# Attention results through DRAM instead of transposes, and a new order of the attention loop

## The chip, the cores and the metric

The kernel runs on one core of one Trainium2 chip. The metric is the device time in microseconds (us) of one execution; lower is better. In the texts PE is the tensor engine, DVE the vector engine, ACT the scalar engine, POOL the GpSimd engine and SP the engine that issues most DMAs.

## The reference

Four layers in a row on one sequence of 2048 rows of 512 values: attention, MLP, attention, MLP, with the same weights both times. Each adds its result to its input, which goes in normalised.

```
def _A_ref(x, wqkv, wo):                 # attention, H = 32 heads of 16
    qkv = (x @ wqkv) ...                 # split into q, k, v by heads
    scores = einsum("bhqd,bhkd->bhqk", q, k) * 16 ** -0.5
    p = softmax(scores)
    o = einsum("bhqk,bhkd->bhqd", p, v)
    return o.reshape(B, S, D) @ wo
def _B_ref(x, w1, b1, w2):               # 512 -> 1792, Mish, -> 512
    ...
x = x + _A_ref(_layernorm(x), A_wqkv, A_wo)
x = x + _B_ref(_layernorm(x), B_w1, B_b1, B_w2)
x = x + _A_ref(_layernorm(x), A_wqkv, A_wo)
x = x + _B_ref(_layernorm(x), B_w1, B_b1, B_w2)
```

## The kernel before, in words

The text speaks of a "layer" for one attention with its MLP; there are two (l = 0 and 1).

**Precision.** Values of large matmuls are split into a high and a low part of a fast format (`mm3`: three matmuls for one product), so weights and activations are stored twice, after a copy and a subtraction ("split"). p x v works on plain float32 tiles.

**The attention loop** (`Attention.run`) goes over 512 steps. A step stands for one block of 512 queries, one tile of 128 keys and four heads. 16 steps (all keys) make a block, four blocks (all queries) a group of four heads, and eight groups all heads. There are 2048 head tiles in a layer, 3 of them to one `p` tile. What is done in a step is listed letter by letter in `CYCLE`, which repeats every three steps:

- P (`pair`): two matmuls give the scores of two head tiles in one two-bank PSUM tile (tag s2, one buffer), and one exp on ACT of 1024 columns writes them to `p`. After each P, `drain` looks whether a block is finished.
- S (`single`): the third head tile, one bank (tag s1, one buffer), an exp of 512 columns.
- M (`max_mm`): half of what one step needs for the row maxima: two matmuls into a PSUM tile of 1024 columns (tag mx, two buffers) and a max reduce on DVE. 1024 halves make a layer. They run ahead of the scores, by 24 steps at the start (`AHEAD`; these are made during the q, k, v projection). At the end of a block `max_fold` and, three steps later, `max_rows` bring the maxima with one transpose on PE into two additional rows of the queries, so that the scores come out shifted.
- v (`pv`): p x v, four heads side by side in 32 columns each of the array, accumulated over the 16 steps of a block in one PSUM bank (tag acc, one buffer). Each head has 32 columns: 16 of v, one of ones (for the sum of p), the rest zero.

PE's instructions are chained in this program order by `pe`. The order on the other engines, and the slots of the pools, are chosen when the program is built by a scheduler with a time model; each engine and the queue of SP then hold their instructions in that order.

**The end of a block.** `drain` copies the accumulator to SBUF on ACT (`ot`, L360). Two steps later `out_rows` transposes it on PE (L368), copies it again, inverts the sums with a pow on POOL (L373) and writes the normalised result to the tiles `ost` (four tiles of 8 KB per partition that stay for the whole attention).

**The tail.** `wo_parts` transposes these tiles (L495), splits them and multiplies by wo, chunk by chunk (a chunk is 512 rows, c = 0 to 3); chunk 0 is spread over the last 24 steps of the loop ("fill"), in PE's chain. Behind the loop follow the other chunks, the splits of the remaining w1 and w2 (`load_w1`, `load_w2`, with `split_load`: a DMA into one of three raw buffers, a copy on DVE, a subtraction on POOL), the norm of the first chunk, and the MLP.

**SBUF.** Nearly all large tiles come from one pool, `blk`, of 22 slots of 8 KB per partition: q and k of a group (four slots), v of a group, the `p` tiles, weights and residuals. A DMA into such a tile waits in SP's queue until its slot is free.

The lines of the profile's code that the change touches:

Of the kernel before, what the change touches and what calls it, by code (L numbers as in the profile page):

```python
# [25 lines left out]
HG = 4  # L26
# [8 lines left out]
HALF = 64  # L35
K_PARTS = (0, 0, 1)
Q_PARTS = (0, 1, 0)
CYCLE = ("PMSvv", "PMSvMPMSv", "PMSvvM")
AHEAD = 24
GSTEPS = NCH * NKT  # L40
STEPS = NG * GSTEPS
# [8 lines left out]
def kernel(ctx: ExitStack, tc: tile.TileContext, x, wqkv, wo, w1, b1, w2, out):  # L50
# [15 lines left out]
    mone = const.tile([P, NCH * HG], F32, name="mone")  # L66
    nc.gpsimd.memset(mone, -1.0)
# [113 lines left out]
    class Attention:  # L181
        def __init__(self, l, scr):
            self.l, self.scr = l, scr
            self.vscr = dram.tile([NG, P, NKT, HG * VW], F32, name=f"vscr{l}")
            self.va = {}
            self.qk, self.mxs, self.pts, self.accs = {}, {}, [], {}
            self.singles, self.full = 0, None
            self.ost = None
            self.later = []
            self.chained, self.running, self.last = False, False, None  # L190

# [133 lines left out]
            self.pe(nc.tensor.matmul(sp, k, q, start=True, stop=True))  # L325
            nc.scalar.activation(self.pts[i // 3][:, 2], sp, AF.Exp, scale=SCALE)  # L326

        def pv(self, i):
            s, half = divmod(i, 2)
            if not 0 <= s < STEPS:  # L330
                return
            b, kt = divmod(s, NKT)
            g, qb = divmod(b, NCH)
            l = self.l
            va = self.va[g]
            if kt == 0 and half == 0:
                self.accs[b] = pbank("acc", f"pv{l}{b}")
            acc = self.accs[b]
            cols = ts(half, CW // 2)
            for h in range(HG):  # L340
                j, e = divmod(s * HG + h, 3)
                self.pe(
                    nc.tensor.matmul(  # L343
                        acc[ts(h, VW), cols],
                        va[:, kt, h, :],
                        self.pts[j][:, e, cols],
                        start=kt == 0 and half == 0,
                        stop=kt == NKT - 1,
                        skip_group_check=True,
                    )  # L350
                )
            if kt == NKT - 1 and half == 1:
                self.full = b

        def drain(self):
            b, self.full = self.full, None
            if b is None:
                return
            ot = t512("f", f"ot{self.l}{b}")
            nc.scalar.activation(ot, self.accs.pop(b), AF.Copy)  # L360
            self.later.append((2, lambda: self.out_rows(b, ot)))

        def out_rows(self, b, ot):
            g, qb = divmod(b, NCH)
            l = self.l
            tp = self.bank(f"otp{l}{b}")
            for t in range(NCH):
                self.pe(nc.tensor.transpose(tp[:, ts(t, P)], ot[:, ts(t, P)], ident))  # L368
            of = t512("f", f"of{l}{b}")
            nc.scalar.activation(of, tp, AF.Copy)  # L370
            ov = of.rearrange("p (t h d) -> p t h d", t=NCH, h=HG)
            rc = tmp.tile([P, NCH, HG, 1], F32, tag="rc", name=f"rc{l}{b}")
            nc.gpsimd.tensor_tensor(  # L373
                rc, ov[:, :, :, DH : DH + 1], mone.rearrange("p (t h o) -> p t h o", t=NCH, h=HG), op=ALU.pow
            )
            nc.gpsimd.tensor_tensor(
                self.ost[qb][:, :, ts(g, HG * DH)].rearrange("p t (h d) -> p t h d", d=DH),
                ov[:, :, :, 0:DH],
                rc.to_broadcast([P, NCH, HG, DH]),
                op=ALU.mult,  # L380
            )

        def run(self, hooks, ost, fill):
            ost.extend(b8([P, NCH, D], F32, f"o{self.l}{c}") for c in range(NCH))
            self.ost = ost
# [36 lines left out]
    def qkv(l, wts, tt, order, late):  # L422
# [65 lines left out]
    def wo_parts(l, c, ost, wot, x2, pe, tail):  # L488
        def rows(t):
            if tail:  # L490
                tp = ps.tile([P, 2, 512], F32, tag="mx", name=f"op{l}{c}{t}")[:, 0]
            else:
                tp = pbank("s", f"op{l}{c}{t}")
            for k in range(KT):
                pe(nc.tensor.transpose(tp[:, ts(k, P)], ost[:, t, ts(k, P)], ident))  # L495
            oh = t512("ah", f"oh{l}{c}{t}", F32R)
            ol = t512("al", f"ol{l}{c}{t}", F32R)
            if tail:
                nc.vector.tensor_copy(oh, tp)
            else:  # L500
                nc.scalar.activation(oh, tp, AF.Copy)
            nc.vector.tensor_tensor(ol, tp, oh.bitcast(F32), op=ALU.subtract)
            return oh, ol

        ready = rows(0)
        yield
        for t in range(NCH):
            oh, ol = ready
            if t % 2 == 0:
                acc = ps.tile([P, 2, 512], F32, tag="mx", name=f"wo{l}{c}{t}")  # L510
            for k in range(KT):
                mm3(
                    acc[:, t % 2],
                    [(oh[:, ts(k, P)], ol[:, ts(k, P)], wot[k // 2][:, 0, k % 2], wot[k // 2][:, 1, k % 2])],
                    first=k == 0,
                    last=k == KT - 1,
                    pe=pe,
                )
                yield
                if k == 0 and t + 1 < NCH:  # L520
                    ready = rows(t + 1)
                    yield
# [88 lines left out]
    for l in range(2):  # L611
# [21 lines left out]
        for i in range(2):  # L633
            hooks[STEPS - GSTEPS + 2 * i] = lambda i=i: wot.append(load_rows(wo, i, f"wo{l}{i}", hi="pool"))
            hooks[STEPS - 40 + i] = lambda i=i: load_res(i)
        for i in range(4):
            hooks[STEPS - GSTEPS + 8 + 2 * i] = lambda i=i: load_w1(i, hi="pool")
        ost = []

        def wo_first():  # L640
            yield from wo_parts(l, 0, ost[0], wot, x2s[0], att.pe, True)

        fill = wo_first()
        att.run(hooks, ost, fill)
# [56 lines left out]
```

## Time and profile before

| | |
|---|---|
| median of 3 runs | 3804.7 us (3803.79 to 3808.43) |
| the profiled execution, its own time | 3797.65 us |
| its span, first to last instruction | 3795.9 us |
| granted PE clock, mean | 0.994 |
| q, k, v projection, layer 0 | to about 200 us |
| attention, layer 0 (first p x v to last) | 207.8 to 1538.1 us |
| wo matmuls, layer 0 | 1470.6 to 1586.2 us |
| MLP, layer 0 (first to last matmul) | 1577.2 to 1932.6 us |
| attention, layer 1 | 2092.5 to 3425.2 us |
| MLP, layer 1 | 3468.2 to 3791.1 us |

The two attentions take 70% of the time. The busy share of an engine over the whole span mixes stages, so what one stage waits for has to be read in that stage. In the groups of instructions, "idle before" is idle time of that engine ahead of the group, with what ended it; idle time of an engine that is not the one all others wait for costs nothing.

### The profile page before, as it was taken

The page shows a single profiled execution, that of the slowest core. Times are in us where ns is not written, and L with a number is a line of the kernel's source. Part 1 is how long each engine was busy: PE and PEld are TensorE (multiplying, and loading weights), DVE is VectorE, ACT ScalarE, POOL GpSimd, SP SyncE. Part 2 cuts the span into 40 slices and gives each one's busy share as a digit, 9 for nine tenths or more (in the row PEclk, how much of TensorE's full clock was granted, in tenths as well). Part 3 has the DMA queues.
Part 4 walks back from the last instruction along what each step waited for, and adds up shares of the span by engine and source line. Part 5 has one row for each costly group of instructions (what it writes and reads, how often), then busy time and mean ns, then how long its engine had stood idle before and what let it go on. Part 6 is the DMA issues. An engine that isn't in the chain of part 4 may idle for free.

```text
span 3795.9 us, 70660 instructions
## 1 busy us (share of the span) xinstructions
PE 3681.6 (97%) x29504; PEld 2050.2 (54%) x29504; DVE 3008.9 (79%) x3010; ACT 2558.6 (67%) x3573; POOL 746.6 (20%) x594
## 2 busy tenths in 40 slices
PE   7999999999999999999999999999999999999999
PEld 5644444444444444687767444444444444447887
DVE  5679999999999995566655899999999999946555
ACT  2178888888888887444431788888888888873444
POOL 1200100100110030444420010010011001305544
PEclk9999999999999999999999999999999999999999
DMA  6530111102011110100055202111020110101000
GB/s 193 178 70 21 27 24 36 27 21 36 22 27 29 31 35 23 62 12 12 28 167 184 40 22 38 19 30 30 18 36 21 32 32 23 57 1 62 12 12 23
DMA packets 108849, 168.16 MB, mean 44 GB/s; under 512 B 13808, under 2 KB 61936, under 8 KB 102384
## 3 DMA queue, kind: packets, MB, share of 16 engines
q1 hardware_dynamic: 86288, 122.73, 14.0%
q10 hardware_dynamic: 22240, 40.90, 3.1%
q8 instruction: 232, 3.80, 0.4%
q14 instruction: 89, 0.73, 0.1%
HBM read 102.77 MB, written 58.72 MB: 43 GB/s over the span
## 4 chain that ended last, share of the span: by engine, by line
PE 83%; ACT 8%; DVE 3%; DMA 2%; POOL 1%; issue 1%; SPq 0%; ACTq 0%; POOLq 0%; DVEq 0%
PE pv L343 25%; PE pm L261 16%; PE sp L315 12%; PE ss L325 8%; ACT p L316 5%; PE h L133 2%; PE mo L135 2%; PE h L135 2%; PE h L134 2%; PE mo L133 2%; PE mo L134 2%; ACT p L326 1%; PE qk L133 1%; PE qk L134 1%; PE qk L135 1%
## 5 line engine op out<-in xcount | busy, mean ns | idle before, releaser
L265 DVE TENSOR_REDUCE mxv<-pm 128x2 f32<-128x1024 f32 x2048 | 2423.4, 1221 | 299.7 <-PE pm L261 292.1
L316 ACT ACTIVATE p<-sp 128x1024 f32<-128x1024 f32 x1366 | 1398.2, 1024 | 454.0 <-PE sp L315 443.3
L343 PE MATMUL pv<-p,va 128*32 128x256 f32 x16384 | 1168.9, 388 | 0.0
L261 PE MATMUL pm<-ks,qs 48*128 48x512 f32 x4096 | 916.1, 446 | 4.4 <-DMA qs<-scr 3.2
L326 ACT ACTIVATE p<-ss 128x512 f32<-128x512 f32 x1364 | 809.5, 593 | 0.0
L343 PEld LDWEIGHTS pv<-p,va 128*32 128x32 f32 x16384 | 393.8, 109 | 564.6 <-issue 426.3
L315 PE MATMUL sp<-qs,ks 50*128 50x512 f32 x2732 | 623.5, 451 | 18.6 <-ACT p L316 9.5
L261 PEld LDWEIGHTS pm<-ks,qs 48*128 48x128 f32 x4096 | 384.9, 185 | 369.1 <-issue 267.9
L325 PE MATMUL ss<-qs,ks 50*128 50x512 f32 x1364 | 551.9, 405 | 5.2 <-ACT of L370 0.6
L373 POOL TENSOR_TENSOR rc<-of,mone 128x16 f32<-128x16 f32 x64 | 186.3, 2912 | 1485.1 <-ACT of L370 1432.6
L315 PEld LDWEIGHTS sp<-qs,ks 50*128 50x128 f32 x2732 | 259.3, 184 | 317.9 <-ACT p L316 266.8
L325 PEld LDWEIGHTS ss<-qs,ks 50*128 50x128 f32 x1364 | 253.9, 186 | 127.9 <-ACT p L326 56.2
L546 POOL TENSOR_TENSOR hb<-hb,he 128x512 f32<-128x512 f32 x112 | 157.5, 1406 | 186.9 <-DVE he L543 180.1
L288 POOL CAST np<-nf 16x128 fp32r<-16x128 f32 x64 | 17.9, 280 | 893.7 <-ACT nf L287 880.1
L549 POOL TENSOR_TENSOR hb<-hb,hr 128x512 f32<-128x512 f32 x112 | 161.1, 1439 | 136.9 <-DVE ah L548 113.3
L133 PE MATMUL mo<-w,ah 128*128 128x512 f32 x448 | 178.9, 399 | 0.8 <-DVE ah L548 0.7
L544 ACT ACTIVATE hr<-he 128x512 f32<-128x512 f32 x112 | 70.9, 633 | 159.5 <-DVE he L543 81.0
L133 PE MATMUL h<-thm,w 128*128 128x512 f32 x448 | 176.1, 393 | 1.4 <-ACT hb L540 1.4
L134 PE MATMUL mo<-w,ah 128*128 128x512 f32 x448 | 176.8, 395 | 0.0
L550 DVE TENSOR_TENSOR al<-hb,ah 128x512 fp32r<-128x512 f32 x112 | 110.8, 989 | 83.1 <-POOL hb L549 80.2
L135 PE MATMUL h<-thm,w 128*128 128x512 f32 x448 | 175.7, 392 | 0.0
L134 PE MATMUL h<-tlm,w 128*128 128x512 f32 x448 | 175.3, 391 | 0.0
(170 smaller groups left out, 2982.0 us busy)
## 6 DMA issues: line engine op xcount, KB each, us to landing
scr<-pt ACTq DMA_DIRECT2D x64, 512.0 KB
qs<-scr SPq DMA_DIRECT2D x192, 128.0 KB
ks<-scr SPq DMA_DIRECT2D x192, 128.0 KB
vscr<-v SPq DMA_DIRECT2D x32, 512.0 KB
va<-vscr SPq DMA_DIRECT2D x64, 256.0 KB
qs<-np SPq DMA_DIRECT2D x512, 2.0 KB
x<-in_A_x_dram SPq DMA_DIRECT2D x7, 1024.0 KB
xs<-x SPq DMA_DIRECT2D x4, 1024.0 KB
```

Of the source, the lines that this page charges most:

```text
L133: pe(nc.tensor.matmul(acc, ah, bh, start=first and i == 0, stop=False))
L134: pe(nc.tensor.matmul(acc, ah, bl, start=False, stop=False))
L135: pe(nc.tensor.matmul(acc, al, bh, start=False, stop=last and i == n - 1))
L261: nc.tensor.matmul(pm[:, e], qs[u][rows, q0 : q0 + P], ks[u][rows, ts(n, 512)], start=True, stop=True)
L265: nc.vector.tensor_reduce(self.mxs[b][:, 2 * u : 2 * u + 2, qt, n], pm, axis=AX.X, op=ALU.max)
L315: self.pe(nc.tensor.matmul(sp[:, e], k, q, start=True, stop=True))
L316: nc.scalar.activation(self.pts[-1][:, 0:n], sp[:, 0:n], AF.Exp, scale=SCALE)
L325: self.pe(nc.tensor.matmul(sp, k, q, start=True, stop=True))
L326: nc.scalar.activation(self.pts[i // 3][:, 2], sp, AF.Exp, scale=SCALE)
L343: nc.tensor.matmul(acc[ts(h, VW), cols], va[:, kt, h, :], self.pts[j][:, e, cols], start=kt == 0 and half == 0, stop=kt == NKT - 1, skip_g ...
L373: nc.gpsimd.tensor_tensor(rc, ov[:, :, :, DH : DH + 1], mone.rearrange("p (t h o) -> p t h o", t=NCH, h=HG), op=ALU.pow)
L549: nc.gpsimd.tensor_tensor(hb, hb, r, op=ALU.mult)
```

## The change

- `CYCLE` gets a new order. p x v is done in four groups per three steps, each of 384 columns (three quarters of 128), where it was done in six halves of 256. A group that crosses from one step to the next is issued in two pieces. At a block's end the group breaks off until the accumulator has been drained, and the next one takes up what was left.
- The list of M changes with the order: `"PMSvv", "PMSvMPMSv", "PMSvvM"` becomes `"PMvSM", "PvMSMPv", "MSMPvMS"`.
- `drain` no longer transposes. The block's raw result (values and sums of four heads) goes to DRAM (`oscr`) by a DMA on SP. All 16 unused columns of a head's v are filled with ones now, so that the sum comes out 16 times, once for each value.
- `heads_out` reads a chunk back with 16 DMAs, in which the heads' dimension lies on the partitions, as the wo matmuls want it: values and sums in two tiles. DVE makes a reciprocal over 2048 columns and a multiply; ACT copies the high part, DVE subtracts for the low part. It is called for chunk 0 at step 482, for chunk 1 at step 503, for chunks 2 and 3 behind the loop.
- `wo_parts` no longer transposes or splits. The four `ost` tiles are gone. One w1 tile instead of four is loaded and split during the attention; the other three follow behind wo's chunk 0, with the high part on DVE.

```diff
-CYCLE = ("PMSvv", "PMSvMPMSv", "PMSvvM")
+CYCLE = ("PMvSM", "PvMSMPv", "MSMPvMS")
+QW = CW // 4
...
+            self.oscr = [dram.tile([KT, 2, P, CW], F32, name=f"oscr{l}{c}") for c in range(NCH)]
...
-        def pv(self, i):
-            s, half = divmod(i, 2)
...
+        def pv(self, upto):
+            while self.unit < min(upto, 4 * STEPS):
+                s, q0 = divmod(self.unit, 4)
+                q1 = min(4, upto - 4 * s)
+                b, kt = divmod(s, NKT)
+                if kt == 0 and q0 == 0:
+                    if self.full is not None:
+                        return
+                    self.accs[b] = pbank("acc", f"pv{self.l}{b}")
+                cols = slice(q0 * QW, q1 * QW)
+                for h in range(HG):
...
+                self.unit = 4 * s + q1
+                if kt == NKT - 1 and q1 == 4:
+                    self.full = b
...
             ot = t512("f", f"ot{self.l}{b}")
             nc.scalar.activation(ot, self.accs.pop(b), AF.Copy)
-            self.later.append((2, lambda: self.out_rows(b, ot)))
-
-        def out_rows(self, b, ot):
...
+            nc.sync.dma_start(self.oscr[qb][g // 2, g % 2], ot)
...
-                for s in range(STEPS + 2):
+                for s in range(STEPS + 4):
...
                         else:
-                            self.pv(done)
                             done += 1
+                            self.pv(3 * done)
...
-                    nc.gpsimd.memset(v, 0.0)
-                    nc.gpsimd.memset(v[:, :, :, DH : DH + 1], 1.0)
+                    nc.gpsimd.memset(v, 1.0)
...
+    def heads_out(l, c, src):
+        nd = []
+        for a in range(2):
+            t = b8([P, KT, CW], F32, f"nd{l}{c}{a}")
+            for hh in range(P // DH):
+                rows = src[c].rearrange("k g (h r) n -> k (g h) r n", r=VW)[:, hh, a * DH : (a + 1) * DH]
+                nc.sync.dma_start(t[ts(hh, DH)], rows.rearrange("k d n -> d k n"))
+            nd.append(t)
+        num, den = nd
+        nc.vector.reciprocal(den, den)
+        nc.vector.tensor_tensor(num, num, den, op=ALU.mult)
+        oh = b8([P, KT, CW], F32R, f"oh{l}{c}")
+        ol = b8([P, KT, CW], F32R, f"ol{l}{c}")
+        nc.scalar.activation(oh, num, AF.Copy)
+        nc.vector.tensor_tensor(ol, num, oh.bitcast(F32), op=ALU.subtract)
+        return oh, ol
...
-        for i in range(4):
-            hooks[STEPS - GSTEPS + 8 + 2 * i] = lambda i=i: load_w1(i, hi="pool")
-        ost = []
+        hooks[STEPS - GSTEPS + 8] = lambda: load_w1(0, hi="pool")
+        outs = {}
...
+        hooks[STEPS - 30] = lambda: finish(0)
+        hooks[STEPS - 9] = lambda: finish(1)
...
         for c in range(NCH):
-            for _ in fill if c == 0 else wo_parts(l, c, ost[c], wot, x2s[c], lambda ins: ins, False):
+            if c + 2 < NCH:
+                finish(c + 2)
+            for _ in fill if c == 0 else wo_parts(l, c, outs, wot, x2s[c], lambda ins: ins):
                 pass
             if c == 0:
-                for i in range(4, 7):
+                for i in range(1, 7):
                     load_w1(i, hi="dve")
```

More of the change, by code (lines that the diff above doesn't have):

```diff
@@ L184, in __init__ @@
             self.vscr = dram.tile([NG, P, NKT, HG * VW], F32, name=f"vscr{l}")
+            self.oscr = [dram.tile([KT, 2, P, CW], F32, name=f"oscr{l}{c}") for c in range(NCH)]
             self.va = {}
             self.qk, self.mxs, self.pts, self.accs = {}, {}, [], {}
-            self.singles, self.full = 0, None
-            self.ost = None
+            self.singles, self.full, self.unit = 0, None, 0
             self.later = []
@@ L326, in single @@
             nc.scalar.activation(self.pts[i // 3][:, 2], sp, AF.Exp, scale=SCALE)
-        def pv(self, i):
-            s, half = divmod(i, 2)
[L330 to L349, printed above, removed]
-                    )
-                )
-            if kt == NKT - 1 and half == 1:
-                self.full = b
+        def pv(self, upto):
[9 more added lines that the diff above has]
+                for h in range(HG):
+                    j, e = divmod(s * HG + h, 3)
+                    self.pe(
+                        nc.tensor.matmul(
+                            self.accs[b][ts(h, VW), cols],
+                            self.va[b // NCH][:, kt, h, :],
+                            self.pts[j][:, e, cols],
+                            start=kt == 0 and q0 == 0,
+                            stop=kt == NKT - 1,
+                            skip_group_check=True,
+                        )
+                    )
+                self.unit = 4 * s + q1
+                if kt == NKT - 1 and q1 == 4:
+                    self.full = b
         def drain(self):
@@ L358, in drain, with run @@
                 return
+            g, qb = divmod(b, NCH)
             ot = t512("f", f"ot{self.l}{b}")
             nc.scalar.activation(ot, self.accs.pop(b), AF.Copy)
-            self.later.append((2, lambda: self.out_rows(b, ot)))
-        def out_rows(self, b, ot):
[L364 to L385, printed above, removed]
+            nc.sync.dma_start(self.oscr[qb][g // 2, g % 2], ot)
+        def run(self, hooks, fill):
             self.prep_v(0)
@@ L486, in qkv, with wo_parts @@
         return att
[L488 to L506, printed above, removed]
+    def heads_out(l, c, src):
[14 more added lines that the diff above has]
+        return oh, ol
+    def wo_parts(l, c, outs, wot, x2, pe):
+        oh, ol = outs[c]
         for t in range(NCH):
-            oh, ol = ready
             if t % 2 == 0:
@@ L519, in wo_parts @@
                 yield
-                if k == 0 and t + 1 < NCH:
-                    ready = rows(t + 1)
-                    yield
             if t % 2:
@@ L635, with finish @@
             hooks[STEPS - 40 + i] = lambda i=i: load_res(i)
-        for i in range(4):
-            hooks[STEPS - GSTEPS + 8 + 2 * i] = lambda i=i: load_w1(i, hi="pool")
-        ost = []
+        hooks[STEPS - GSTEPS + 8] = lambda: load_w1(0, hi="pool")
+        outs = {}
+        def finish(c):
+            outs[c] = heads_out(l, c, att.oscr)
+        hooks[STEPS - 30] = lambda: finish(0)
+        hooks[STEPS - 9] = lambda: finish(1)
         def wo_first():
-            yield from wo_parts(l, 0, ost[0], wot, x2s[0], att.pe, True)
+            yield from wo_parts(l, 0, outs, wot, x2s[0], att.pe)
         fill = wo_first()
-        att.run(hooks, ost, fill)
+        att.run(hooks, fill)
         for c in range(NCH):
-            for _ in fill if c == 0 else wo_parts(l, c, ost[c], wot, x2s[c], lambda ins: ins, False):
+            if c + 2 < NCH:
+                finish(c + 2)
+            for _ in fill if c == 0 else wo_parts(l, c, outs, wot, x2s[c], lambda ins: ins):
                 pass
             if c == 0:
-                for i in range(4, 7):
+                for i in range(1, 7):
                     load_w1(i, hi="dve")
```

4 lines of the change are left out of this document (1 added, 3 removed).

## The prediction

> **What bounds the kernel now.** I read the page first, then the table by stage, the groups and the timeline. The sums are made against the profiled execution (3797.65 us, a span of 3795.9 us and 1.75 us around it); the median of the runs is 7 us above it, and I add those at the end.
>
> ```profile
> PE 3681.6 (97%) x29504; PEld 2050.2 (54%) x29504; DVE 3008.9 (79%) x3010; ACT 2558.6 (67%) x3573; POOL 746.6 (20%) x594
> ```
> ```profile
> 400.00:1200.00 800.00, 786.65 (x7521) 366.68 (x7513) 732.64 (x638) 646.19 (x883) 80.74 (x76) 1.00 0.15 27
> ```
> ```profile
> L265 DVE TENSOR_REDUCE mxv<-pm 128x2 f32<-128x1024 f32 x2048 | 2423.4, 1221 | 299.7 <-PE pm L261 292.1
> L373 POOL TENSOR_TENSOR rc<-of,mone 128x16 f32<-128x16 f32 x64 | 186.3, 2912 | 1485.1 <-ACT of L370 1432.6
> ```
>
> The second line is 800 us of attention: columns are PE, weight loads, DVE, ACT, POOL, clock. PE is busy 98% at full clock, but DVE 92%, so two engines stand within a few per cent of the bound. Its 638 DVE instructions are 619 reduces (one fold, L276, per 32), so 1.29 us per reduce and 7.76 us per three steps of six reduces. How close can reduces stand?
>
> ```profile
> 829.08 0.61 ACT L360 ACTIVATE ot<-pv 128x512 f32<-128x512 f32 x1
> ...
> 829.55 1.05 ACT L316 ACTIVATE p<-sp 128x1024 f32<-128x1024 f32 x1
> 829.74 1.07 PE L343 MATMUL pv<-p,va 128*32 128x256 f32 x16
> ...
> 831.28 2.36 DVE L265 TENSOR_REDUCE mxv<-pm 128x2 f32<-128x1024 f32 x2 [0.41 <-PE pm L261]
> ...
> 833.15 0.66 PE L368 MATMUL otp<-ident,ot 128*128 128x128 f32 x4 [0.20 <-ACT p L326]
> ...
> 839.92 5.95 DVE L265 TENSOR_REDUCE mxv<-pm 128x2 f32<-128x1024 f32 x5 [0.34 <-PE pm L261]
> ```
>
> A pair of reduces takes 2.36 us, five 5.95, one alone 1.22: the next starts 1.14 us (2.36-1.22) to 1.18 us ((5.95-1.22)/4) after the one before. Where no max is left, the score bank sets the pace:
>
> ```profile
> 1528.96 1.02 ACT L316 ACTIVATE p<-sp 128x1024 f32<-128x1024 f32 x1 [0.17 <-PE sp L315]
> ...
> 1530.65 1.02 ACT L316 ACTIVATE p<-sp 128x1024 f32<-128x1024 f32 x1 [0.17 <-PE sp L315]
> ```
>
> One P every 1.69 us: a pair's scores wait for its bank until the exp before has ended.
>
> **Part 1: seven maxes per three steps.** The new CYCLE holds 4 P, 4 S, 4 v, and 2+2+3 = 7 M where the old one held 6. The 1024 halves of a layer start 48 ahead as before, so 976 are left, and they are used up at 976x3/7 = step 418 of 512 (the old list: step 488). PE would need little more: v stays six sets of matmuls, 1536 columns and four changes in and out; one M adds 0.24 us, the output transposes go (0.66 us and some 0.5 us of waits per 16 steps, 0.2 us per three steps). So PE can keep 7.8 us. DVE cannot: 7 x (1.17 + 0.007 for folds) = 8.24 us. Each M has two buffers, and PE's order is fixed, so PE waits at M and everything behind it waits. Steps 0 to 418: 976 x 1.177 = 1149 us.
>
> **Part 2: the drain.** Before, ACT's copy of a finished block (L360) stands ahead of the exp of the next P, as at 829.08, and the new block's first matmul lost at most 0.4 us (20.7 us over 60). In the built order of the changed kernel the copy stands behind that exp in all 64 blocks, and three of four v follow P at once. From P: 0.55 us to the exp, 0.92 until the copy starts, 0.60 for it, 0.05 to PE: v starts at 2.12 us, where it would have at 0.33. Behind the waiting v stand S and the next M; DVE has at most two buffers, 2.36 us of work, and M arrives 3.3 to 4.2 us after the last one, so it idles 1.0 to 1.8 us, 1.4 on average. 26 blocks end before step 418: 37 us. Steps 0 to 418 then take 1186 us; before, read from the first exps, 201.8 to 1285.4, 1083.6 us. **+102** (1.14 us and no drain loss: +36; 1.20 and 1.8 us: +142).
>
> **Part 3: steps 418 to 478.** No max is left: 80 P at 1.69 us are 135 us, four drains at 1.8 us (nothing absorbs them) 7; before, 155. **-13** (-20 to 0). That it gains so little is the point: DVE's work was pressed into 418 steps, and these end on ACT's bank.
>
> **Part 4: the results' way through DRAM.** Removed: 64x4 transposes, copies and POOL's pow and multiply (off the path), and in the tail 32x4 transposes at 0.60 us, 19 us. Added per chunk: 16 loads, a reciprocal over 2048 columns, a multiply, ACT's copy, a subtract. Loads: six short ones take 3.74 us to issue, 0.62 each, big ones 0.37; 16 are 6 to 10 us and some 2 to land: D = 10. Multiply and subtract are twice the 1024-column add (L525, 1223 ns), 2.45 us each; the copy twice a 1024-column exp, 2.1: 7 us. The reciprocal R has no row. Same engine and shape: 2.45 us. The only inversions are POOL's pow, 2912 ns for 16 columns, 66 times its multiply per column (L546, 1406 ns for 512), but on another engine with an exponent tensor; I take 8 us, near DVE's rows.
>
> Chunk 0: its loads wait for slots free at step 477; its copy stands in ACT's queue after step 483, some 15 us later. 10+8+2.5 come 5.5 us late, with all exps behind it. Steps 478 to 500: 29 P are 50 us, two drains 3.6, the wo matmuls of the fill (0.89 us a set, eight sets) 8, the wait 5.5: 67 against 63.4. **+3** (R=2.45: -2).
>
> Chunks 1 to 3 form one chain in the built order. Chunk 1's loads wait for the step-500 p x v; its copy holds ACT at step 503, its 48 wo matmuls stand in PE's queue among the last steps. Chunk 2's loads take a slot that these matmuls free, and seven of them stand in SP's queue behind the last block's drain. Then DVE and POOL split w1 and w2: SP's next loads wait for POOL's raw buffers, and chunk 3's loads stand behind seven of POOL's splits, 2.4 to 2.9 us each. From step 500: D+R+7; wo of chunk 1 and three P 16; rest of the attention 17; seven loads 6; R+7; seven splits 20; D+R+7; wo of chunk 3 and the norm 13: 113+3R = 137 us to the MLP. Before: 1503.9 to about 1583, 79. The cover that hid such latencies was the transposed tiles already in SBUF. **+58** (R=2.45: +41).
>
> The memset change and the w1 loads moved out of the attention lie on POOL, idle there; their cost is the 20 us above. The MLP and qkv stages keep their instructions: nothing.
>
> **Sum.** 102-13+3+58 = 150 us per layer, 300 in both: 3797.65+300+7 = 4105 us.
>
> **Rivals.**
> [...]
> *The chain is hidden*: loads run ahead, the splits overlap. Then +102-13-2+10 = 97 per layer: 3999. For it: SP idles through the attention. Against it: the slot and queue order above.
> *Faster*: PE stays the pace. Then the transposes' 64x1.15 and 19 us come off: 3712. It decides at 7.72/7 = 1.10 us per reduce; the shortest distance read is 1.14.
> *The change doesn't do as it says*: groups even only inside a block; at its end one of 128 columns and one of up to 640. That is in part 2.
>
> **Chances.** Forecast 0.46, repeated division 0.35, chain hidden 0.15, faster 0.04. The forecast's own range is 3990 (R=2.45, reduces near 1.14) to 4170; the repeated division reaches 4250 with reduces at 1.20. Low end 3950: chain hidden with faster reduces. A measurement of this kernel tells some 0.2% (7.6 us) from no change: faster 0.04, same 0.01, slower 0.95.
>
> **What would show it.** DVE near 98% until step 418, 1.14 to 1.20 us between reduces, then none; p x v waiting for ot some 1.8 us per block, 64 times; a reciprocal's row; SP's loads for the last chunk waiting for POOL. Wrong: PE waiting for mxv no more than the 84 us of now, or the MLP starting within 80 us of step 500.

## The result, and the profile after

The changed kernel takes 4229.2 us (median of 4 runs, 4205.12 to 4235.6; a fifth run took 4164.99) where the kernel before took 3805.5 in the same session. Two of the five runs lie over 1.5% above the fastest and count as slow; the three others against the runs of before give the ratio of 1.1033, with a 95% interval of 1.093 to 1.1136. The forecast was 4105, slower, with a range to 4250: the side was right, the size was over a quarter too small. The profiled execution is the one of 4205.12 us, its span 4203.3, so 407.4 us over the span before. Its page, and the window that answers to the one shown of before (columns after the length: PE, weight loads, DVE, ACT, POOL, granted clock, DMA share, GB/s):

```profile
span 4203.3 us, 69190 instructions
...
PE 3801.0 (90%) x28784; PEld 2012.5 (48%) x28784; DVE 3083.0 (73%) x3000; ACT 2596.0 (62%) x3493; POOL 514.5 (12%) x443
...
PEclk9969999999999978699999699999999999886999
...
L264 DVE TENSOR_REDUCE mxv<-pm 128x2 f32<-128x1024 f32 x2048 | 2360.7, 1217 | 195.6 <-PE pm L260 172.8
...
L260 PEld LDWEIGHTS pm<-ks,qs 48*128 48x128 f32 x4096 | 427.3, 188 | 654.9 <-DVE mxv L264 526.9
...
L473 DVE RECIPROCAL nd<-nd 128x2048 f32<-128x2048 f32 x8 | 103.6, 12953 | 337.4 <-DMA nd<-oscr 185.7
```

```profile
400.00:1200.00 800.00, 767.66 (x7076) 339.28 (x7074) 779.00 (x698) 618.13 (x813) 15.82 (x44) 1.00 0.18 36
```

Two lines of before that answer to these, the wait for mxv and the clock row:

```profile
PEld pm L261 <- DVE mxv L265: 84.4, 360, 1.0
```

```profile
PEclk9999999999999999999999999999999999999999
```

In the middle of the loop DVE is busy 97% (92% before) and PE 96% (98%): the bound has moved to DVE, and PE's wait for mxv has grown from 84.4 to 526.9 us. But the clock row shows a second thing, which no step of the forecast had: of its 40 slices not only those of the two tails (15 to 17, 35 to 37) are under 9, but also 3 and 23, each the start of an attention; in the page of before all 40 are 9. And a reciprocal takes 12.95 us.

The time by stage, from the starts of the exps of the pairs (us; where a step falls between two pairs, in proportion; "MLP" is its first activation):

| stage | layer 0 before | after | layer 1 before | after | forecast of the difference |
|---|---|---|---|---|---|
| steps 0 to 24 | 63.3 | 96.1 (+32.8) | 63.3 | 95.9 (+32.6) | in the next row |
| steps 24 to 418 | 1020.3 | 1086.0 (+65.7) | 1021.4 | 1085.9 (+64.5) | +102 with 0 to 24, 37 of it drain |
| steps 418 to 478 | 155.3 | 136.6 (-18.7) | 155.3 | 136.8 (-18.5) | -13 |
| steps 478 to 500 | 62.4 | 92.9 (+30.5) | 62.4 | 84.5 (+22.1) | +3 |
| step 500 to the MLP | 81.2 | 178.9 (+97.7) | 85.8 | 176.7 (+90.9) | +58 |
| the rest | | +4.5 | | +3.3 | 0 |

The sums are +212.5 and +194.9, against a forecast of 150 each. Three rows need a cause: the first 24 steps, and the two of the tail.

**The first 24 steps.** The same window of both kernels, after first and then before (columns as above):

```profile
210.00:220.00 10.00, 10.00 (x63) 4.53 (x62) 6.13 (x6) 4.77 (x6) 0.00 (x0) 0.50 0.01 3
```

```profile
210.00:220.00 10.00, 10.00 (x95) 4.67 (x93) 8.61 (x8) 7.37 (x10) 0.00 (x0) 0.92 0.16 23
```

PE is busy all of both windows, but does 63 matmuls in the one and 95 in the other: its clock stands at 0.50. In both kernels the clock is halved at the loop's start, where the first steps have no p x v yet; before it came back after 6.8 us, after it took 81.9 us, in each layer alike. (The trace records the clock in multiples of 3.4 us, called stretches in what follows; only the end of the program cuts one short.)

**The tail.** Chunk 0 in the changed kernel, from the timeline:

```profile
1517.71 9.73 SPq L470 DMA_DIRECT2D nd<-oscr  x16
...
1535.47 12.95 DVE L473 RECIPROCAL nd<-nd 128x2048 f32<-128x2048 f32 x1 [152.09 <-DMA nd<-oscr]
1548.45 2.29 DVE L474 TENSOR_TENSOR nd<-nd,nd 128x2048 f32<-128x2048 f32 x1
1550.83 1.91 ACT L477 ACTIVATE oh<-nd 128x2048 fp32r<-128x2048 f32 x1 [21.38 <-DVE nd L474]
1552.64 1.01 ACT L315 ACTIVATE p<-sp 128x1024 f32<-128x1024 f32 x1
...
1553.70 0.28 PEld L314 LDWEIGHTS sp<-qs,ks 50*128 50x128 f32 x2 [23.72 <-ACT p L315]
```

The mechanism is the one of the forecast: the copy stands in ACT's queue, all exps behind it. The sizes are not: 17.8 us from the first issue to the last landing (forecast 10), 12.95 for the reciprocal (8), so ACT waits 21.4 us instead of 5.5, and PE 23.7. In this idle time PE's clock falls to 0.50, for 47.8 us in layer 0 and 27.3 in layer 1. At the end the last chunk's loads stand behind the weights' loads in SP's queue, as forecast:

```profile
1714.07 0.40 SPq L103 DMA_DIRECT2D w104r<-in_B_w_dram  x1
...
1730.83 0.37 SPq L103 DMA_DIRECT2D w203r<-in_B_w_dram  x1
1731.29 0.42 SPq L595 DMA_DIRECT2D x<-in_A_x_dram  x1
1731.76 12.84 SPq L470 DMA_DIRECT2D nd<-oscr  x16
```

### The profile page after: what moved, and what is told of

It reads as the page before. It is cut to its first block, busy times and chain, and to the rows that moved or that the text cites. A ratio compares the mean times of both kernels' runs of the same rounds, so it can differ in the third digit from the quotient of the medians.

```text
span 4203.3 us, 69190 instructions
## 1 busy us (share of the span) xinstructions
PE 3801.0 (90%) x28784; PEld 2012.5 (48%) x28784; DVE 3083.0 (73%) x3000; ACT 2596.0 (62%) x3493; POOL 514.5 (12%) x443
## 5 line engine op out<-in xcount | busy, mean ns | idle before, releaser
L264 DVE TENSOR_REDUCE mxv<-pm 128x2 f32<-128x1024 f32 x2048 | 2360.7, 1217 | 195.6 <-PE pm L260 172.8
L340 PE MATMUL pv<-p,va 128*32 128x128 f32 (+3 forms) x16048 | 1204.2, 403 | 0.0
L260 PE MATMUL pm<-ks,qs 48*128 48x512 f32 x4096 | 1102.7, 489 | 73.2 <-DVE mxv L264 68.1
L314 PE MATMUL sp<-qs,ks 50*128 50x512 f32 x2732 | 707.0, 441 | 52.3 <-ACT p L315 50.6
L260 PEld LDWEIGHTS pm<-ks,qs 48*128 48x128 f32 x4096 | 427.3, 188 | 654.9 <-DVE mxv L264 526.9
L324 PE MATMUL ss<-qs,ks 50*128 50x512 f32 x1364 | 609.0, 446 | 0.0
L314 PEld LDWEIGHTS sp<-qs,ks 50*128 50x128 f32 x2732 | 304.2, 191 | 175.7 <-ACT p L315 145.4
L473 DVE RECIPROCAL nd<-nd 128x2048 f32<-128x2048 f32 x8 | 103.6, 12953 | 337.4 <-DMA nd<-oscr 185.7
L132 PE MATMUL wo<-wo,oh 128*128 128x512 f32 x128 | 60.9, 476 | 185.9 <-ACT oh L477 185.9
L132 PE MATMUL mo<-w,ah 128*128 128x512 f32 x448 | 176.9, 395 | 1.6 <-DVE ah L520 1.5
L134 PE MATMUL mo<-w,al 128*128 128x512 f32 x448 | 161.9, 400 | 17.2 <-DVE al L522 17.0
```

Source lines behind the costliest of these rows:

```text
L132: pe(nc.tensor.matmul(acc, ah, bh, start=first and i == 0, stop=False))
L134: pe(nc.tensor.matmul(acc, al, bh, start=False, stop=last and i == n - 1))
L260: nc.tensor.matmul(pm[:, e], qs[u][rows, q0 : q0 + P], ks[u][rows, ts(n, 512)], start=True, stop=True)
L264: nc.vector.tensor_reduce(self.mxs[b][:, 2 * u : 2 * u + 2, qt, n], pm, axis=AX.X, op=ALU.max)
L314: self.pe(nc.tensor.matmul(sp[:, e], k, q, start=True, stop=True))
L340: nc.tensor.matmul(self.accs[b][ts(h, VW), cols], self.va[b // NCH][:, kt, h, :], self.pts[j][:, e, cols], start=kt == 0 and q0 == 0, stop ...
```

## The experiments

All are edits of one of the two kernels, each one execution with its profile unless a ratio is given. The five runs of the unedited changed kernel lie up to 71 us apart, and the lower a run's clock the longer it took (0.955 for 4164.99 us, 0.944 for 4205.12, 0.936 for 4226.83 and more); so a single run is read by its stages, and its span is given beside them. The theories: the loop is paced by DVE because of the seventh M (the forecast's), or the groups of 384 themselves cost; the half clock follows the even spread of p x v, or PE's waits; the tail is a chain of loads and reciprocals, or these lie beside other work.

**The order of p x v, with seven M.**

```diff
-CYCLE = ("PMvSM", "PvMSMPv", "MSMPvMS")
+CYCLE = ("PMSvvM", "PMSMPM", "SvvMPMS")
```

> The changed kernel with another order of the same items: still seven M, four P, four S and four v per three steps, but v in adjacent pairs (768 columns in a row) instead of evenly spread. Question: why do the first 24 steps of each layer take 96.1 us (before 63.3), with the granted clock at 0.50 for 81.9 us although PE is busy all the time. Theory A (the clock returns only when much p x v falls into one stretch of 3.4 us; the even spread never gives that, only the 640 columns in a row at the first block's end do): the clock returns after one to four stretches of 3.4 us, as before, and steps 0 to 24 take 66 to 72 us; the span falls by 50 to 60 us, to about 4145 to 4155. Theory B (the seventh M does it: PE waits for DVE and so is not busy enough): 96 us again, span 4190 to 4215. Both: 8.24 to 8.3 us per three steps after that.

Measured: a span of 4917.3 us, and 10.1 to 10.9 us per three steps up to step 408. Both theories missed: in this order PE and ACT wait for each other's single buffers (in 800 us ACT waited 275 us for sp, PE was busy 672), so it tells nothing of DVE. On the clock it tells something: it falls some eighty times in each layer's loop, as PE now idles often, but most times returns after a single stretch of 3.4 us, and up to step 400 never takes longer than 10.2. In the changed kernel, with p x v spread evenly and PE busy 80.3 of the 81.9 us, it took all of these.

**Six M instead of seven.** First one M was struck out of the list, then the six were placed evenly:

```diff
-CYCLE = ("PMvSM", "PvMSMPv", "MSMPvMS")
+CYCLE = ("PMvS", "PvMSMPv", "MSMPvMS")      # first run
+CYCLE = ("PMvSM", "PvMSPM", "vSMPvMS")      # second run
```

> The changed kernel with one M less in CYCLE: six M per three steps, p x v still in even groups of 384. It undoes the heavier demand on DVE alone. Theory A of the prediction (DVE paces steps 0 to 418 at seven M): three steps fall from 8.27 us to PE's own pace, 7.6 to 7.8 us, M lasts until step 488, steps 418 to 478 go back from 136.6 to about 153 us; per layer 24 to 418 falls by 60 to 85 us and 418 to 478 rises by 15 to 18, so the span falls by 90 to 140 us. Rival (the groups of 384 themselves cost PE time, DVE only waits with it): three steps stay above 8.0 us and the span falls by less than 40. On the clock at the loop's start: if the even spread of p x v holds it down, it stays at 0.50 for tens of us here too (steps 0 to 24 at 85 to 100 us); if the seventh M does, it returns after some 7 us (63 to 68 us).

Measured: 4187.1 us, only 16 less; 8.05 us per three steps. Five of its six M stand close together, and the list of waits for 400 to 1200 us (us in total, times, longest) shows DVE and PE waiting for each other in turn:

```profile
PEld pm L260 <- DVE mxv L264: 163.5, 359, 0.8
...
DVE mxv L264 <- PE pm L260: 112.3, 107, 2.2
```

So this run did not separate the theories: its M come in bunches, which two buffers did not even out. It did answer the question on the clock: with six M steps 0 to 24 took 85.4 us in both layers, 61.4 of them at half clock, so the seventh M is not what holds the clock down. Hence the second run:

> The changed kernel with six M per three steps, evenly placed (in the run with six before this one, five of the six stood within 5 us of each other: DVE waited 112 us for pm and PE 163 us for mxv). Theory A (DVE's order alone held that run at 8.05 us per three steps; without it PE sets the pace): 7.6 to 7.8 us, 24 to 418 takes 998 to 1024 us, 418 to 478 some 153, span 4090 to 4125. Theory B (the groups of 384 and their order cost PE or ACT time whatever M does): 8.0 us or more, span 4170 to 4195.

```profile
400.00:1200.00 800.00, 790.24 (x7677) 356.22 (x7678) 756.73 (x669) 673.96 (x905) 14.54 (x40) 1.00 0.18 36
```

7.42 us per three steps, below every expectation: PE is busy 99% again, and 24 to 417 takes 972 us (before 1018, changed kernel 1084). The DVE theory holds: the seventh M costs 0.85 us per three steps, 112 us up to step 417 (1084 - 972), of which 13 come back from step 418 to 478 (136.6 us with seven, 149.2 with six); without it the new loop gains 45 us a layer on the old one. These are figures of layer 0. The span fell only to 4103.5, as expected by the sum but not in its parts: the tails are the same, and in layer 1 the clock stayed at 0.50 for the first 287 us.

**The two halves of the loop's change on the kernel before.** A seventh M alone, and the grouping alone (with `pv` of the change, the transposes and the tail as before):

```diff
-CYCLE = ("PMSvv", "PMSvMPMSv", "PMSvvM")
+CYCLE = ("PMSvMv", "PMSvMPMSv", "PMSvvM")   # first run
+CYCLE = ("PMvSM", "PvMSPM", "vSMPvMS")      # second run, groups of 384
```

> The kernel before, with one M more in its CYCLE (seven per three steps) and nothing else: p x v in halves, output transposes and tail as before. Theory A (DVE paces seven M): 8.24 to 8.3 us per three steps until step 418, then 6.75 to 7.0; per layer +66 and -14 to -18, the span rises by 95 to 105 us, to about 3895. Theory B (DVE's 8% of idle time takes most of it): 7.8 to 8.05 us, span 3800 to 3850.

Measured: 4209.0 us, four times the loss expected. Where the clock is full, mostly 8.46 to 8.70 us per three steps, so somewhat over DVE's pace, with PE and DVE each waiting for the other. And the clock is at 0.50 for 345 us of layer 0: steps 312 to 336 took 13.8 us per three. The seventh M is a loss on either kernel, and the half clock needs no groups of 384; the added M also stands between two halves of p x v that were adjacent before.

> The kernel before, its output transposes and tail kept, with the even groups of 384 and six evenly placed M per three steps. This is the grouping alone. Theory A (four long groups instead of six short ones save PE some changes in and out, 0.05 to 0.1 us each): 7.55 to 7.72 us per three steps instead of 7.77, 10 to 35 us less per layer in the loop. Theory B (the order, not PE, costs): 7.85 us or more. On the clock both expect what the even spread did so far: 0.50 for 55 to 82 us at each layer's start, 20 to 33 us more per layer. Span 3780 to 3845 by A, over 3850 by B.

Measured: 3850.3 us, 7.65 us per three steps: the grouping with its order gains 0.12, as theory A said, and taking the output transposes away another 0.23 (7.65 to 7.42; the forecast had 0.2). Steps 0 to 24 took 96.0 and 92.8 us, at half clock for 85 and 78. Of the 54 us over the span before, these starts are +62, the loop from 24 to 417 is -31, its end from 477 to the MLP +16, and 7 lie behind layer 0's MLP begin.

**What brings the clock back.** In the changed kernel most stretches of 3.4 us at half clock held the same share of p x v, 0.42 of PE's time: one group of 384 each (some held 0.55). In six of the nine cases of the runs so far (the changed kernel, six M, and the wide loads and the missing reciprocal below) it came back 3 to 6 us after a block's copy to `ot`, where the broken-off group stands with the next, up to 640 columns in a row. In two of the others, of the first run with six M, it came back behind a stretch with 0.65 or more, though an earlier one with 0.65 had not brought it back. So p x v of four steps (3 to 6) was held back and done in one piece:

```diff
                             done += 1
-                            self.pv(3 * done)
+                            if not 3 <= s < 7:
+                                self.pv(3 * done)
```

> The changed kernel, but p x v of the steps 3 to 6 of each layer is held back and then done in one piece at step 7 (2304 columns in a row, 5 to 6 us at half clock). Everything after step 7 keeps the even groups. Theory A (what brings the clock back is a stretch of 3.4 us that is mostly p x v; in the runs so far it came back 3 to 6 us after a block's copy, where 640 columns stand together, and stayed at 0.50 for 82 us while each stretch held the same share, 0.42, of p x v): the clock is at 0.50 for 27 to 41 us instead of 81.9, steps 0 to 24 take 72 to 80 us instead of 96, and the span falls by 30 to 50 us to 4155 to 4175. Theory B (time, or the end of a block itself, brings it back): 82 us and 96 us again, span 4195 to 4215.

```profile
200.00:210.00 10.00, 9.49 (x32) 4.61 (x31) 9.69 (x9) 7.86 (x11) 0.00 (x0) 0.54 0.74 152
210.00:220.00 10.00, 9.96 (x38) 4.00 (x39) 8.59 (x9) 6.89 (x9) 0.00 (x0) 0.50 0.00 1
220.00:230.00 10.00, 9.03 (x78) 3.39 (x70) 5.75 (x5) 4.04 (x6) 0.00 (x1) 0.94 0.01 2
230.00:240.00 10.00, 9.71 (x93) 4.34 (x95) 9.29 (x9) 7.63 (x10) 0.72 (x2) 1.00 0.42 66
```

20.5 and 17.1 us at half clock, steps 0 to 24 in 71.4 and 71.1 us, span 4137.5: theory A, and more than it said. Of the 60 us by which the two starts lay over DVE's pace (8 x 8.25 = 66 us for 24 steps) this gives back 49. The burst returns in three kernels below: in all eight starts of these four kernels the clock came back while the burst ran, 14 to 21 us after it had fallen, where the sixteen starts of the kernels with seven M or with groups of 384 and no burst (the run with pairs aside) took 37.5 to 287 us. The opposite was tried too: as much PE work without a wait, but of M's kind.

```diff
+                    if s == 7:      # 24 more matmuls of 48 rows, 512 columns
+                        fp = self.bank(f"fp{self.l}")
+                        for n in range(24):
+                            self.pe(nc.tensor.matmul(fp, qs[0][0:KROWS, 0:P], ks[0][0:KROWS, 0:512], start=True, stop=True))
```

> The changed kernel with 24 additional matmuls at step 7 of each layer, of the kind that M makes (48 rows, 512 columns; nothing reads them): some 10 us at half clock in which PE never waits. p x v keeps its even groups. Theory A (the gate counts something of which p x v has much and these matmuls little, rows in use or the like): the clock stays at 0.50 until the first block's end, 80 to 95 us, and steps 0 to 24 take 97 to 108 us; span 4205 to 4225. Theory B (any stretch without a wait brings it back): 0.50 for 25 to 45 us, steps 0 to 24 in 75 to 85 us; span 4165 to 4190.

```profile
225.00:232.00 7.00, 7.00 (x17) 5.42 (x17) 0.43 (x2) 0.00 (x0) 0.00 (x0) 0.50 0.00 0
```

PE was busy without a gap for two whole stretches of 3.4 us, and the clock stayed at 0.50, for 92.2 us in layer 0. In layer 1 it came back after 47.8 us, 15 us behind the last of them. Steps 0 to 24 took 106.7 and 89.4 us: theory A in layer 0, between the two in layer 1. So PE's busy time alone did not bring the clock back here. That it is something of which p x v (all 128 rows, four column groups at once) has more than matmuls of 48 rows fits the burst, but is argued and not shown. What it is stays open: some returns came at a share of 0.42, as in layer 1 of the run with wide loads (37.5 us, its start not edited), and stretches with 0.55 passed without one.

**The loads.**

```diff
-            for hh in range(P // DH):
-                rows = src[c].rearrange(...)[:, hh, a * DH : (a + 1) * DH]
-                nc.sync.dma_start(t[ts(hh, DH)], rows.rearrange("k d n -> d k n"))
+            for k in range(KT):
+                rows = src[c].rearrange(...)[k, :, a * DH : (a + 1) * DH]
+                nc.sync.dma_start(t[:, k], rows)
```

> The changed kernel with the 16 loads of a chunk (16 partitions each) replaced by 8 loads that write 128 partitions each (one per tile and k); the bytes and the 2 KB pieces are the same. Theory A (a load into 16 partitions is slow: its 2 KB packets took 217 to 236 ns, all others of this size 86 to 95): packets fall to about 90 ns, issue to landing from 17.5 us to 8 to 10, ACT's wait at chunk 0 from 21.4 to 12 to 14 us, and 8 us each at four chunks make 25 to 35 us per layer; span 4135 to 4160. Theory B (reading raw outputs row by row from DRAM sets it): packets and landing stay, within 2 us; span 4195 to 4215.

Measured: 2 KB packets of 88 to 100 ns on average instead of 217 to 236, as theory A said. But issue to reciprocal fell only from 17.4 to 13.6 us at chunk 1 (the second line; the first is chunk 0), and ACT's wait at chunk 0 from 21.4 to 18.8:

```profile
1524.12 5.37 SPq L470 DMA_DIRECT2D nd<-oscr  x8
...
1608.30 5.33 SPq L470 DMA_DIRECT2D nd<-oscr  x8
```

The reciprocal of chunk 1 starts at 1621.87. The packets of eight loads need 5.6 us on 16 engines (1024 x 88 ns / 16), and took 11.8 from first to last: with wide loads it is not the packets that set the time. What does was not followed up. From step 478 to the MLP: 250.2 and 252.6 us against 271.8 and 261.2, 15 us a layer where theory A had 25 to 35. That the span (4163.6) still comes within 4 us of theory A's range is the clock's doing: layer 1's start took 17 us less (37.5 us at 0.50 instead of 81.9).

**The reciprocal.**

```diff
-        nc.vector.reciprocal(den, den)
```

> The changed kernel without the reciprocal (the product is taken with the denominator itself, so its outputs are not the reference's). Theory A (the chunks form one chain and each reciprocal of 12.95 us lies on it): 13 us at chunk 0 and 3 times 13 from step 500 to the MLP, 52 per layer; span 4095 to 4110. Theory B (the chain is set by the loads and by POOL's splits, the reciprocals lie beside them): 13 to 26 us per layer, span 4150 to 4180.

From step 478 to the MLP: 213.9 and 209.7 us, 58 and 52 less: theory A. ACT's waits for the four products of layer 0, which were 21.4, 22.6, 24.5 and 56.7 us, are now 6.6, 9.4, 11.4 and 45.1, each 11 to 15 shorter. The reciprocals were on the path all four times. The span (4147.2) fell by 56, not by 110, as the clock was low at other places here: for 51 us in the middle of layer 0's loop, until 6 us behind a block's copy, and for 150 at layer 1's start.

```profile
1048.00:1098.00 50.00, 50.00 (x276) 22.00 (x277) 30.25 (x26) 24.15 (x31) 0.72 (x2) 0.50 0.08 28
```

**Versions that put it together.** First the kernel before with the grouping (six M, as above) and the burst at step 7; then the changed kernel with all causes mended:

> The kernel before with the even groups of 384, six evenly placed M (as the last run), and p x v of steps 3 to 6 done in one piece at step 7. Theory A (the 55 us that the last run lost against the kernel before are the clock at the two layers' starts, 96 and 93 us for 24 steps against 63, and the loop itself gains 0.12 us per three steps): with the clock back after 20 to 30 us, 24 steps take 64 to 70 us and the span falls by 48 to 62 us to 3788 to 3802, level with the kernel before or up to 0.3% below. Theory B (the clock also falls in the middle of the loop in some executions): the median lies 10 to 40 us above the profiled span.

Measured: 3791.6 us against 3805.1, ratio 0.9957 (0.994 to 0.9974). Steps 0 to 24 took 66.2 and 66.0 us, half clock 17.1 each. The kernel is 0.4% faster than the one before. Four runs lay within 5 us, each with a mean granted clock of 0.990 or 0.991: theory A.

```diff
+        nc.scalar.activation(den, den, AF.Ln)
+        nc.scalar.activation(den, den, AF.Exp, scale=-1.0)
-        nc.vector.reciprocal(den, den)
...
+        hooks[STEPS - 42] = lambda: fetch(0)              # the loads alone
+        hooks[STEPS - 26] = lambda: finish(0)
+        hooks[STEPS - 24] = lambda: fetch(1)
+        hooks[STEPS - 8] = lambda: (finish(1), fetch(2))
...
+                fetch(3)                                  # behind the loop, ahead of the weights
+                finish(2)
+                finish(3)
```

> The changed kernel with the five causes found mended, and its outputs still by way of DRAM: six evenly placed M (7.42 us per three steps in the run with these), the burst at step 7, loads of 128 partitions, 1/x as exp(-ln x) on ACT (two passes of some 1.9 us instead of 12.95 us on DVE), and each chunk's loads issued 12 to 16 steps ahead of their use, chunk 3's ahead of the weights. Theory A (these were the causes): steps 0 to 24 in 65 to 72 us, 24 to 480 in 1128 to 1140 (before 1180), from step 480 to the MLP 150 to 185 us (before 139, changed kernel 267); per layer 1343 to 1397 against 1383, so 3660 to 3825 us, most likely 3730 to 3770: the first version of this change that is faster. Theory B (a chain through DRAM at the layer's end cannot be hidden): from step 480 over 210 us, and 3850 or more.

Measured: 3819.6 us, ratio 1.0026 (1.0007 to 1.0046), so not faster. The loop keeps 7.42 us, the tail from 478 takes 194.7 and 192.8 us; counted from 480 it is 186 and 184, beyond theory A's 150 to 185 or at its edge, and far from theory B's 210. Two waits were left. On ACT the logarithm of chunk 0 had been placed ahead of its data; the first line is the window in which PE lost 4.5 us by it and by the two passes that follow it on ACT, the second what came after:

```profile
1370.00:1376.00 6.00, 1.49 (x11) 0.37 (x3) 2.22 (x2) 4.62 (x4) 0.00 (x0) 0.94 0.66 229
1376.00:1415.00 39.00, 37.97 (x214) 16.13 (x214) 23.05 (x18) 19.55 (x26) 1.56 (x2) 0.50 0.01 1
```

This hole of a few us was followed by 75 us at half clock. And at the end PE stood behind DVE's weight casts:

```profile
1570.31 1.11 PE L167 MATMUL tpm<-ident,xnm 128*128 128x128 f32 x4 [31.16 <-DVE tlm L127]
```

The next version moved these casts to POOL, w1 and w2 in turn, loaded x's last chunks ahead of them, and pinned the logarithm behind its loads:

```diff
+                load_res(2)
+                load_res(3)
...
-                for i in range(1, 7):
-                    load_w1(i, hi="dve")
-                for i in range(4):
-                    load_w2(i, hi="dve")
+                for i in (1, 2, -1, 3, -2, 4, -3, 5, -4, 6):
+                    load_w1(i, hi="pool") if i > 0 else load_w2(-i - 1, hi="pool")
...
+        pin = tc.keep_in_program_order if c < 2 else lambda ins: ins
```

> The last run's kernel with three waits of its tail taken away: (1) PE stood 31.2 us at each layer's end because the first norm's subtracts stood on DVE behind ten weight casts, which wait for SP's loads: these casts go to POOL, w1 and w2 in turn, and x's last two chunks are loaded ahead of them; (2) the logarithm of chunks 0 and 1 stood on ACT 2 to 7 us ahead of its data, and the 5.5 us that PE lost there were followed by 75 and 72 us at half clock: it is held at its place in the program, 14 steps behind its loads. Theory A (these are what is left): steps 24 to 477 in 1118 to 1126 us (1131), from step 477 to the MLP 140 to 165 us (last run 199, before 146); span 3690 to 3745. Theory B (POOL's casts and splits, some 3.8 us for each of ten tiles, are the bound ahead of the MLP, or the clock falls all the same): 175 to 200 us from step 477, span 3765 to 3810.

```profile
1385.00:1566.00 181.00, 147.13 (x1019) 79.80 (x1016) 76.84 (x79) 101.07 (x117) 44.22 (x26) 0.88 0.22 78
```

Measured: 3764.1 us against 3802.6, ratio 0.9906 (0.9889 to 0.9923): 0.9% faster than the kernel before, by more than the interval. The span, 3761.8, lies between the two theories. Steps 24 to 477 took 1120.5 us (theory A), without the 75 us at half clock, but 477 to the MLP 180.4 (theory B's 175 to 200): PE is busy 147 of 181 us there at a clock of 0.88, where before it was busy 139 of 146 at 1.00. The way through DRAM still costs 31 to 34 us a layer at its end; the loop, 53 us a layer shorter than before from 24 to 477, pays for it.

## Why the forecast was right in sign and too small

By its own parts; the gap is 407 - 300 = 107 us in the span. The result lies inside the stated range (3950 to 4250) but above the forecast's own part of it (3990 to 4170): the upper end was there for a reciprocal of 18 us and reduces 1.20 apart, and neither came. What filled that room was the clock, a term that the forecast did not have (+65), and the tail, put too low (+119), less the drain that did not come (-74).

**Part 1, seven maxes: right.** 24 to 418 takes 8.27 us per three steps (forecast 8.24); a run of eleven reduces takes 12.73 us, 1.15 apart ((12.73 - 1.22) / 10), between the 1.14 and 1.18 read before:

```profile
799.76 12.73 DVE L264 TENSOR_REDUCE mxv<-pm 128x2 f32<-128x1024 f32 x11
```

The even run with six M shows it by its absence. PE's own pace was put a little too high: the 7.42 us measured with six M and the forecast's 0.24 for one more make some 7.66 (an estimate), where it said that PE "can keep 7.8 us".

**Missing in it: the clock, +65 us.** Steps 0 to 418 took 98.5 and 97.1 us more than before; the pace's share was 65.4. The forecast read the clock only in its middle window, at 1.00. The trace of before shows it at 0.50 for 6.8 us at each loop's start; that a kernel whose PE is busy 80.3 of 81.9 us could stay there that long was in no rival. The burst gives back 49 of the 65. So the close hit of this row, 102 forecast and 98.5 and 97.1 measured, is luck: the pace's 65 came, the drain's 37 did not, and the clock put 32 to 33 in its place.

**Part 2, the drain: wrong, -74 us.** The 1.4 us times 26 blocks did not come. The block's end in the timeline of the changed kernel:

```profile
809.58 0.63 PE L314 MATMUL sp<-qs,ks 50*128 50x512 f32 x2
...
810.14 0.42 PE L340 MATMUL pv<-p,va 128*32 128x128 f32 x8
810.30 1.03 ACT L315 ACTIVATE p<-sp 128x1024 f32<-128x1024 f32 x1
...
811.22 0.59 ACT L359 ACTIVATE ot<-pv 128x512 f32<-128x512 f32 x1
...
812.08 0.16 PEld L340 LDWEIGHTS pv<-p,va 128*32 128x32 f32 x8 [0.37 <-ACT ot L359]
```

The copy does stand directly behind an exp, but behind that of the P ahead of the block's last 128 columns, not of the P after it. The step took "behind an exp" for "behind the next P". By the time the next group wants the bank, at 811.7, two M, an S and another P have kept PE and DVE busy; the wait is 0.37 us here and 9.5 us in all, 28 times.

**Part 3: right, the gain a little small, -11 us.** 136.7 us against 142: the four drains of 1.8 us were not there either.

**Part 4, chunk 0: mechanism right, sizes wrong, +47 us.** D was made of 16 issues; the bytes were not priced. The row was in the trace of before: q and k go into 16 partitions at a time too, in 8 KB packets of 0.88 us (median), and 2 MB at that pace are 14 us (256 packets x 0.88 / 16). With the issue of the first and the landing of the last that is the 17.5 measured. R was 12.95 and not 8. With both, ACT's 5.5 us become 5.5 + 7.8 + 5 = 18.3 of the 21.4 measured; the rest of the stage lies in the half clock behind it, when a P of layer 0 came every 2.59 us where the bank's pace is 1.69.

**Part 4, the chain: mechanism right, sizes wrong, +72 us.** Three reciprocals of 12.95 (+15 a layer) and two whole loads of 17.5 (+15) explain 30 of the 36 us a layer. Without its reciprocals the tail lost 58 and 52 us, which is all four in a row (4 x 12.95 = 51.8). The remaining 6 were not separated; the clock, 0.73 from 1516 to 1790 us where it was 1.00 before, is the likely cause.

**The stages between:** +8, where 0 was said; +7.1 of it lies between layer 0's MLP begin and layer 1's first exp. It was not followed up.

**The rivals.** The repeated division, with its chance of 0.35 and the range's upper end of 4250, stood on R = 18, eight passes at a row's pace of 2.28 us. No run shows the eight passes; in their place the trace shows 12.95 us, 5.7 times the multiply's 2.29. That lies in the middle between the forecast's 8 and the rival's 18, so it decides for neither. "The chain is hidden" and "faster" did not come true; the run with six even M shows how near "faster" was in the loop, and what stood against it: the tail and the clock.

**The median** lies 24 us above the profiled execution, not 7: the three other runs of the four had a mean granted clock of 0.936 against its 0.944, and the fifth run, of 4164.99 us, had 0.955. With this kernel the time of a run goes with its clock, which the forecast, made for one clock, could not hold.

## What to carry to other kernels

Spread the demand on the second engine evenly and keep it under its pace: with two buffers between them, one M in seven too many cost 112 us a layer up to step 417, more than the PE time that the new order had freed. Before results are sent through DRAM at a stage's end, price the packets' own times for the number of partitions written (here 217 to 236 ns into 16, 88 to 100 into 128), and put the loads many steps ahead of the instruction that waits for them, since everything on that engine's queue waits too (here ACT 21.4 us and PE 23.7). Look at the granted clock at each stage's first microseconds: behind a hole of a few microseconds (PE busy 1.5 of 6 us) a PE that was busy nearly all the time (38.0 of the next 39 us) stayed at half its clock, here for 75 us, and at the loop's start a burst of p x v was followed by its return, 14 to 21 us after the fall, in eight starts of eight.

## What the runs showed of the hardware

- PE's granted clock stayed at 0.50 for 82 us, of which PE was busy 80.3, and in one run for 287; after 7 us of back-to-back matmuls of 48 rows it was still 0.50, with bursts of p x v on all rows (2304 columns in one piece) it came back, in eight starts of eight. The records of the clock are multiples of 3.4 us.
- A DVE reciprocal of 128x2048 f32 takes 12.95 us, 6.3 ns per column, 5.7 times a multiply (2.29). A logarithm and an exp of that size on ACT take 1.91 each.
- Loads into 16 partitions: 2 KB packets of 217 to 236 ns on average, 115 to 157 GB/s in the middle of chunk 0's loads; into 128 partitions 88 to 100 ns, though a chunk's loads took 11.8 us and not the 5.6 of their packets.
